# Chunk-select attention and a gated feed-forward on one core: the first group of gate weights in one transfer, 56 constant matmuls for 30, and a new order for the first 24 microseconds

## The chip, the core and the metric

The kernel runs on one core of one Trainium2 chip. A core has five engines with queues of their own: TensorE (PE, matmul; its weight loads are listed as PEld and overlap with the matmuls), VectorE (DVE), ScalarE (ACT), GpSimd (POOL) and SyncE (SP, which here only issues transfers). The metric is the device time of the program in microseconds, where less is better. A profiled execution also gives the start and the length of every instruction.

## What is computed

The first half is attention in which each query sees only the six best of the 24 chunks of 32 keys, chosen by an upper bound from each chunk's smallest and largest key. The second half is a feed-forward with a sigmoid gate. The shapes are B = 4, H = 8, S = 768, D = 64; then 3072 tokens of 512 numbers with 1536 hidden ones.

```python
k_min = np.min(k_chunks, axis=3)
k_max = np.max(k_chunks, axis=3)
ub = np.sum(np.maximum(q[:, :, :, None, :] * k_min[:, :, None, :, :], q[:, :, :, None, :] * k_max[:, :, None, :, :]), axis=-1)
ub = np.where(causal, ub, -1000000000.0)
top_chunks = np.argsort(ub, axis=-1)[..., -top_k:]
scores = scale * np.matmul(q, k.transpose(0, 1, 3, 2))
...
scores = np.where(mask, scores, -1000000000.0)
...
attn = attn / (np.sum(attn, axis=-1, keepdims=True) + 1e-09)
return np.matmul(attn, v).astype(np.float32)
...
gate = 1.0 / (1.0 + np.exp(-(x @ w_gate)))
val = x @ w_val
return (gate * val @ w_out).astype(np.float32)
```

## The kernel before, in words

Tokens are handled in eight units, `u0` to `u7`, of 384 rows. `u0` holds the first block of 128 rows of batches 0, 1 and 2 (the fourth batch's first block comes later, in `u2`). In these blocks every query sees at most four chunks, so the function `first` computes plain causal attention for them. The units from `u1` on go through the choice of chunks (`choose`) and the attention over them (`attend`); `ffn` follows for each. The attention of one unit is interleaved with the feed-forward of the unit before it.

Nothing is scheduled while the program runs or by a compiler. Each piece of work is recorded with `plan.add` under a name, with the buffers that it reads and writes. A hand-written table, `ORDER` (from L96), lists all names in sequence, with the letter of the engine after each (`P`, `A`, `V`, `G`, `S` for PE, ACT, DVE, GpSimd and SyncE); each engine executes its own entries in that sequence, and a piece that must wait holds up all that stands behind it on its engine. `SLOTS` gives every buffer its place: PSUM has eight banks, so each tile there waits until the last reader of the bank's former tile is done. `TIES` has entries `a<b`: piece `a` waits for piece `b`, on another engine, though no data goes between them.

These names are used later on, in the order in which the work flows:

- `fl_*` (`keep_awake`, L589 to L595): a matmul of a constant tile with itself, 128 x 256. Nothing reads its result. `ones16` (L587) is its input.
- `kfT_b`, `qfT_b` (L709): four transposes each, which turn the keys and queries of block b; `kf16_b`, `qf16_b` cast the result (the helper `copy`: L452 on ACT, L454 on DVE, L456 on GpSimd). `scf` (L746) are the block's scores, `expf` (L751) the exponentials, `cmf` (L753, GpSimd) the causal mask, `pvf` (L760) the product with the values, `rzf` and `xf` (L766, L768, DVE) the division, `xpsf` (L775) the transposes back and `xTf` the copies into `xT_u0`, which `u0`'s feed-forward reads. `vc_b` casts the values of block b.
- For `u1`: `kn`, `qn` copy the landed keys and queries (`kq_u`) into the layout for turning, `kT`, `qT` (L795) turn them, and `kt`, `qf`, `hk`, `hq` are copies and casts of these. `kx0`, `kx1` (L681) and `kxf` (L719) take the smallest and the largest key of each chunk, and `kcr_u1`, `kcr_f` (L688) finish the ranges; `qm` (L695) is the positive part of the queries. `ub_u1` (L896, tiles `ube`, `ubo`) multiplies queries with ranges and so needs all of `qf`, `qm` and `kcr` of the unit.
- `epat` (L561, L566) is a pattern that marks the chunk of each key; eight copies of it (`hkp000` to `hkp111`, 64 x 1536) fill the rows next to the keys, so that the score matmul adds the mask of the chosen chunks.
- `wgp` (L610), `wg0` to `wg2` (L612), `wv0` to `wv2` (L613) and `wo0` to `wo2` (L618) are transfers of the weights, cast to 16 bits on the way, all issued by GpSimd on the queue that the profile calls q0. The inputs are issued by SyncE on q1. A group of weights is 512 columns of hidden numbers, 512 KB as the profile counts it; `wgp` is its first quarter of rows, in one transfer ahead of the other three quarters.
- `g_u0_*`, `v_u0_*` (L1259) are the feed-forward matmuls of `u0`, four to a piece, one for each quarter of the rows. `tanh` (L1271) makes the gate and `hg` (L1280) the product of the two.

The work around the change is the front: it runs from the first instruction to the point where `g_u0` and `ub_u1` have started. SyncE's order there is `k2_u1`, the keys and queries of the first blocks, the other keys and queries of `u1`, then `v_0_3`, `v_0_2`, `v_0_1`, and then the loads of `u2` and of the fourth first block.

## Time and profile before

| | us |
|---|---|
| three runs of the kernel before | 279.79, 280.38, 280.73 |
| median of these | 280.38 |
| the profiled execution, its own time | 279.88 |
| span of the profile, first to last instruction | 278.2 |

The span is 1.68 us under the profiled execution's own time, which also holds what lies around the first and the last instruction. Times in the profile count from the start of the span. A line of a timeline or of the chain reads: start, duration, engine, source line, operation, output and input, number of instructions in the run; in brackets, how long the engine was idle before it and what released it. In a line of groups the busy time and the mean duration of one in ns stand after the bar. In the lines of the DMA queues the columns are packets, MB and the share of the 16 DMA engines' time. A last column at a transfer is the time from its issue to its landing.

### The profile page before, as it was taken

The numbers are of one execution on the slowest core, as the hardware profiler recorded it, in microseconds if no ns is written. First come the engines' busy times: TensorE is split into PE (matmuls) and PEld (weight loads), VectorE is DVE, ScalarE is ACT, GpSimd is POOL, SyncE is SP. The second block draws the span as 40 slices with busy tenths as digits, with TensorE's granted clock in tenths as the row PEclk, the third lists the DMA queues.
The fourth block names the chain that finished last, engine by engine and source line by source line (L and its number), as shares of the span: only waits on it lengthen the run. The fifth ranks groups of instructions, "written<-read, shape, count | busy, mean of one in ns | idle before, by whom it ended". The sixth has DMA issues, their size and how long they took to land.

```text
span 278.2 us, 7566 instructions
## 1 busy us (share of the span) xinstructions
PE 269.2 (97%) x2806; PEld 189.3 (68%) x2806; DVE 231.2 (83%) x686; ACT 180.4 (65%) x386; POOL 163.1 (59%) x262
## 2 busy tenths in 40 slices
...
GB/s 157 258 281 204 207 217 208 220 179 202 187 217 189 142 183 188 145 161 125 164 157 114 68 85 17 40 0 3 73 77 2 1 83 127 2 1 2 151 2 152
DMA packets 131717, 34.70 MB, mean 125 GB/s; under 512 B 119776, under 2 KB 128736, under 8 KB 131680
## 3 DMA queue, kind: packets, MB, share of 16 engines
...
q8 instruction: 22, 0.36, 0.5%
q14 instruction: 15, 0.12, 0.1%
...
## 4 chain that ended last, share of the span: by engine, by line
PE 87%; DMA 6%; DVE 5%; SPq 1%; issue 0%; POOL 0%; DVEq 0%
PE v_u L1259 20%; PE g_u L1259 15%; PE sc_u L957 12%; PE o_u L1308 11%; PE p_u L1082 10%; PE pv_u L990 7%; DMA wg<-in_moe_w_gate_dram 5%; PE p_g_u L1191 5%; PE ube_u L896 3%; DMA kf<-in_k_dram 1%; DVE xf L768 1%; PE kfT L709 1%; PE qfT L709 1%; PE fl L591 1%; DVE kx_u L681 1%; DVE kcr L681 1%
## 5 line engine op out<-in xcount | busy, mean ns | idle before, releaser
L968 ACT ACTIVATE att_u<-sc_u 128x512 f16<-128x512 f32 (+3 forms) x184 | 86.9, 573 | 8.6 <-PE sc_u L957 7.3
L1259 PE MATMUL v_u<-xT_u,wv 128*128 128x384 f16 x384 | 72.4, 326 | 0.0
L1280 DVE SCALAR_TENSOR_TENSOR hg_u<-gate_u,v_u 128x384 f16<-128x384 f16 x96 | 51.2, 545 | 19.3 <-ACT gate_u L1271 9.7
L1271 ACT ACTIVATE gate_u<-g_u 128x384 f16<-128x384 f32 x72 | 35.1, 499 | 40.3 <-PE g_u L1259 35.1
L1259 PE MATMUL g_u<-xT_u,wg 128*128 128x384 f16 x288 | 56.0, 326 | 0.9 <-ACT xT_u L452 0.5
L1259 PEld LDWEIGHTS <-wv 128*128 128x128 f16 x384 | 36.2, 98 | 20.3 <-issue 0.2
L974 POOL TENSOR_SCALAR_AFFINE_SELECT att_u<-att_u 128x384 f16<-128x384 f16 (+1 forms) x56 | 28.0, 509 | 37.4 <-ACT att_u L968 16.4
L1259 PEld LDWEIGHTS <-wg 128*128 128x128 f16 x288 | 26.7, 98 | 18.3 <-DMA wg<-in_moe_w_gate_dram 1.8
L1308 PE MATMUL o_u<-wo,hg_u 128*128 128x512 f16 x144 | 34.3, 379 | 0.0
L990 PE MATMUL pv_u<-v,att_u 128*128 128x65 f16 x640 | 26.3, 193 | 0.0
L990 PEld LDWEIGHTS <-att_u 128*128 128x128 f16 x640 | 24.2, 98 | 2.9 <-issue 0.6
L1228 DVE TENSOR_TENSOR f_g_u<-p_g_u,f_g_u 128x192 f32<-128x192 f32 (+1 forms) x72 | 24.9, 383 | 1.0 <-PE p_g_u L1191 0.4
L957 PE MATMUL sc_u<-hqe,hke 128*128 128x128 f16 (+2 forms) x220 | 25.1, 243 | 0.0
L957 PE MATMUL sc_u<-hqo,hko 128*128 128x128 f16 (+2 forms) x220 | 24.1, 243 | 0.0
L1308 PEld LDWEIGHTS <-hg_u 128*128 128x128 f16 x144 | 13.7, 98 | 13.4
L957 PEld LDWEIGHTS <-hke 128*128 128x128 f16 x220 | 16.5, 98 | 4.9 <-issue 0.6
L957 PEld LDWEIGHTS <-hko 128*128 128x128 f16 x220 | 16.4, 98 | 4.4
L673 POOL CAST v<-v 128x512 f16<-128x512 f32 x23 | 14.4, 627 | 5.8 <-DVE qf_u L863 1.8
L1271 ACT ACTIVATE gate_u<-f_g_u 128x384 f16<-128x384 f32 x24 | 11.9, 519 | 5.6 <-DVE hg_u L1280 2.9
L1011 DVE TENSOR_TENSOR x_u<-pv_u,rz_u 128x384 f16<-128x384 f32 (+1 forms) x28 | 14.6, 524 | 0.9 <-DMA xT_u<-x_u 0.6
L919 DVE MAX8 mx_u<-ubn_u 128x8 f32<-128x8 f32 (+16 forms) x152 | 12.7, 158 | 0.3
L1099 DVE SCALAR_TENSOR_TENSOR sw<-p_u,sw 128x256 f32<-128x256 f32 (+1 forms) x20 | 10.6, 528 | 2.4 <-PE p_u L1082 2.0
...
## 6 DMA issues: line engine op xcount, KB each, us to landing
...
qf<-in_q_dram SPq DMA_DIRECT2D x8, 128.0 KB, 3.3
```

The lines of the kernel that those rows point to most:

```text
L673: plan.add(f"v16_{b}_{ib}", {POOL: pool(H * D)}, lambda e: nc.gpsimd.tensor_copy(v16[b % 2][:, ib, :, 0:D], at(t)), reads=[t], writes=[("v ...
L957: nc.tensor.matmul(at(t)[:, o:o + 128 * m], hk[b % 2][e_][:, p, 128 * jb:128 * jb + 128], hq[u.side][e_][:, p, 128 * x:128 * (x + m)], sta ...
L968: plan.add(f"exp_{u.name}_{h}_{y}", {ACT: act(n)}, lambda e, t=t, att=att, b0=b0, n=n: nc.scalar.activation(at(att)[:, b0:b0 + n], at(t), ...
L974: nc.gpsimd.affine_select(out=dv, in_=dv, compare_op=ALU.is_ge, fill=0.0, base=0, pattern=[[0, u.m], [1, 128]], channel_multiplier=-1)
L990: nc.tensor.matmul(at(pv)[:, last, x, :], at(att)[:, c:c + 128], v16[b % 2][:, jb, h, :], start=(jb == 0), stop=(jb == ib))
L1011: plan.add(f"x_{u.name}_{p}", {DVE: dve(u.t)}, lambda e: nc.vector.tensor_tensor(at(x_).rearrange("p a (e d) -> p e a d", e=2), at(pv)[:, ...
L1082: nc.tensor.matmul(at(to)[:, side], a(j)[:, i], b(j)[:, i], start=j == i == 0, stop=j == 2 and i == 1)
L1228: plan.add(f"{p}_{name}", {POOL: pool2(192 * n), DVE: dve(192 * n)} if slow else {DVE: dve(192 * n)}, lambda e: both(e).tensor_tensor(dst( ...
L1259: nc.tensor.matmul(at(t), w16[:, c, 128 * fb:128 * fb + 128], at(u.xt)[:, c, :], start=(c == 0), stop=(c == 3))
L1271: plan.add(f"tanh_{u.name}_{fb}", {ACT: act(T, not seven[0])}, lambda e, gv=gv, gate=gate: nc.scalar.activation(at(gate), gv(), AF.Tanh, s ...
L1280: plan.add(f"hg_{u.name}_{fb}", {DVE: dve(T)}, lambda e, vv=vv, gate=gate, hg=hg, fb=fb: nc.vector.scalar_tensor_tensor(at(hg)[:, fb % 2], ...
L1308: nc.tensor.matmul(at(o), at(hgs[fc // 2])[:, fc % 2, 128 * tb:128 * tb + 128], wo16[:, fc, lo:hi], start=(fc == 0), stop=(fc == NFB - 1))
```

## The change

In the code, the loop that records the constant matmuls runs to 56. `wgp` is gone: `wg0` brings all four quarters, and the first four `g` pieces of a unit wait for it alone.

```diff
@@ -592,7 +596,7 @@
             at(t), ones16, ones16.unsqueeze(1).to_broadcast([128, 2, 128]), start=True, stop=True),
             reads=["ones16"], writes=[t], prio=-9.0)
 
-    for i in range(30):
+    for i in range(56):
         keep_awake(i)
     const("ident16", {DVE: (150, 230)}, lambda e: nc.vector.tensor_copy(ident16, ident32),
           reads=["ident32"], writes=["ident16"], prio=-1.0, port=True)
@@ -604,13 +608,8 @@
 
     def weights(i, prio, after):
         lo, hi = 512 * i, 512 * i + 512
-        c0 = 0
-        if i == 0:
-            c0 = 1
-            plan.add("wgp", {POOL: (760, 760)}, lambda e: nc.gpsimd.dma_start(wg16[:, 0:1, lo:hi], wgs[:, 0:1, lo:hi]),
-                     writes=[("wg", 0, "first")], prio=prio, dma=(750, 2048))
-        return plan.add(f"wg{i}", {POOL: (760, 760)}, lambda e: nc.gpsimd.dma_start(wg16[:, c0:, lo:hi], wgs[:, c0:, lo:hi]),
-                 reads=after, writes=[("wg", i)], prio=prio, dma=(750 * (4 - c0), 2048)), plan.add(f"wv{i}", {POOL: (760, 760)}, lambda e: nc.gpsimd.dma_start(wv16[:, :, lo:hi], wvs[:, :, lo:hi]),
+        return plan.add(f"wg{i}", {POOL: (760, 760)}, lambda e: nc.gpsimd.dma_start(wg16[:, :, lo:hi], wgs[:, :, lo:hi]),
+                 reads=after, writes=[("wg", i)], prio=prio, dma=(3000, 2048)), plan.add(f"wv{i}", {POOL: (760, 760)}, lambda e: nc.gpsimd.dma_start(wv16[:, :, lo:hi], wvs[:, :, lo:hi]),
                  reads=after, writes=[("wv", i)], prio=prio, dma=(3000, 2048))
 
     def weights_out(i, prio, after):
@@ -1265,7 +1264,7 @@
             else:
                 g = ps(f"g_{u.name}_{fb}", "ff", [128, T])
                 gv, gk = lambda g=g: at(g), [g]
-                op = plan.add(f"g_{u.name}_{fb}", pe(650), product(g, wg16), reads=xt + [("wg", fb // 4)] + [("wg", 0, "first")] * (fb < 4), writes=[g],
+                op = plan.add(f"g_{u.name}_{fb}", pe(650), product(g, wg16), reads=xt + [("wg", fb // 4)], writes=[g],
                               prio=next_())
                 plan.hold(op, gate)
             plan.add(f"tanh_{u.name}_{fb}", {ACT: act(T, not seven[0])}, lambda e, gv=gv, gate=gate: nc.scalar.activation(
```

The rest of the change lies in the three tables. In `ORDER` the entries up to the first score matmul of `u1` stand in a new sequence, here with the entries of before first; the 1770 behind them are the same, on the same engines. Of the pieces that both have, 25 change their engine; among them `hkp000` goes from ACT to DVE, `hkp100` from GpSimd to DVE, `hkf0` from GpSimd to ACT, `kf16_0`, `qf16_1` and `qf16_2` from DVE to ACT, and `kcr_f` from DVE to GpSimd. `hkp111` stays on ACT and moves to the end of this part. SyncE's transfers keep their sequence.

```diff
-ident=G ones16=V fl_4=P fl_2=P fl_8=P fl_3=P fl_1=P fl_0=P fl_29=P k2_u1=S kn_u1_2=A qf1_0=S kf1_0=S kf0_0=S fl_6=P fl_5=P epat0=V
-ident16=V ap0=V epat=G hkp110=A hkp000=A hkp001=V kT_u1_2=P kcr0=V kt_u1_2=V hk0_u1_2=G vf1_1=G hkp011=V hkp010=G vf1_2=G hkp100=G
-kf1_2=S kf0_1=S kfT_0=P kxf1=V fl_17=P fl_10=P fl_7=P kx0_u1_2=V kf16_0=V qf0_0=S qfT_0=P qf16_0=V qf1_1=S kf1_1=S kfT_1=P
-kf16_1=V fl_15=P fl_16=P scf_0=P expf_0_1=A fl_19=P qf0_1=S qfT_1=P hq0=V ap1=V fl_14=P fl_9=P fl_13=P fl_11=P fl_18=P fl_12=P
-qf16_1=V scf_1=P v10=G vf_0=S v16_0_0=G qf0_2=S qf1_2=S kf0_2=S expf_0_0=A cmf_0_0=G pvf_0_0=P rzf_0_0=V xf_0_0=V kx1_u1_2=V
-cmf_0_1=G wgp=G kfT_2=P pvf_0_1=P qfT_2=P qf16_2=V rzf_0_1=V xf_0_1=V kxf0=V expf_1_0=A cmf_1_0=G vf_1=S vc_1=G pvf_1_0=P
-rzf_1_0=V xpsf_0_0=P expf_1_1=A cmf_1_1=G pvf_1_1=P hkf0=G hk1_u1_2=A kf16_2=A scf_2=P expf_2_1=A expf_2_0=A k0_u1=S kn_u1_0=V
-kT_u1_0=P xf_1_0=V fl_20=P fl_21=P wg0=G q3_u1=S qn_u1_3=A q2_u1=S rzf_1_1=V xf_1_1=V xpsf_1_1=P hq1=V xTf_1_1=V kx0_u1_0=V
-kx1_u1_0=V vf_2=S wv0=G cmf_2_0=G fl_23=P xpsf_0_1=P fl_24=P fl_22=P fl_27=P xpsf_1_0=P vc_2=G xTf_1_0=V pvf_2_0=P rzf_2_0=V
-xf_2_0=V q1_u1=S k3_u1=S kn_u1_3=G kT_u1_3=P hkp111=A q0_u1=S fl_28=P kx1_u1_3=V cmf_2_1=G pvf_2_1=P xpsf_2_0=P rzf_2_1=V xf_2_1=V
-qT_u1_3=P qf_u1_3=V k1_u1=S qn_u1_1=A qT_u1_1=P xTf_0_0=A xTf_0_1=A qn_u1_2=A qn_u1_0=A kn_u1_1=G kT_u1_1=P kx1_u1_1=V kx0_u1_1=V
-kt_u1_0=A qm_u1_3=A fl_25=P xpsf_2_1=P fl_26=P qT_u1_2=P v_0_3=S v_0_2=S v_0_1=S qf1_3=S k0_u2=S q2_u2=S k1_u2=S qf_u1_1=V
-qf_u1_2=V v11=G wv1=G wg1=G hq0_u1_3=G qT_u1_0=P kt_u1_3=A hk0_u1_3=G hq1_u1_3=G wv2=G xTf_2_1=A xTf_2_0=A qf_u1_0=A qm_u1_0=A
-g_u0_0=P g_u0_2=P kx0_u1_3=V kcr_f=V kcr_u1=V hkp101=V hq1_u1_0=V hkf1=V kt_u1_1=V hk0_u1_1=G wg2=G qm_u1_2=A qm_u1_1=A ub_u1=P
-ubn0_u1=V ubm0_u1=V hq0_u1_1=A hq0_u1_2=A g_u0_3=P g_u0_1=P mx0_u1=V ap0_u1=V apt0_u1=V hqm0_u1_0=V v_u0_1=P v_u0_0=P v_u0_2=P
-hq0_u1_0=A tanh_u0_2=A tanh_u0_1=A hg_u0_1=V ubn1_u1=V v_u0_3=P tanh_u0_3=A hg_u0_3=V ubm1_u1=V hg_u0_2=V tanh_u0_0=A hg_u0_0=V
-hk0_u1_0=A hq1_u1_1=A sc_u1_0_2=P exp_u1_0_2=A sc_u1_1_2=P sc_u1_0_1=P sc_u1_0_0=P exp_u1_1_2=A sc_u1_1_0=P sc_u1_1_1=P
...
+ones16=V fl_17=P fl_6=P fl_15=P fl_39=P fl_36=P fl_2=P fl_14=P fl_33=P fl_31=P fl_34=P fl_5=P fl_10=P fl_32=P fl_1=P fl_35=P
+fl_19=P fl_16=P fl_21=P fl_7=P fl_3=P fl_0=P fl_37=P fl_30=P fl_4=P fl_13=P k2_u1=S qf1_0=S kf1_0=S kf0_0=S fl_54=P fl_27=P
+ident=G kfT_0=P ap1=V kcr0=V epat0=V epat=G hkp110=A hkp010=G hkp001=V hkp011=V vf1_1=G v10=G kf1_2=S kf0_1=S kf16_0=A qf0_0=S
+fl_9=P fl_8=P fl_29=P qfT_0=P qf16_0=V fl_52=P fl_47=P kn_u1_2=G kT_u1_2=P kx1_u1_2=V kt_u1_2=V hk0_u1_2=V ident16=V qf1_1=S
+kf1_1=S kfT_1=P hkf0=A scf_0=P expf_0_1=A expf_0_0=A cmf_0_0=G qf0_1=S fl_46=P qfT_1=P fl_50=P qf16_1=A fl_48=P fl_11=P fl_24=P
+fl_12=P fl_38=P vf_0=S v16_0_0=G qf0_2=S qf1_2=S qfT_2=P qf16_2=A kf0_2=S kf16_1=V fl_40=P scf_1=P fl_18=P pvf_0_0=P ap0=V
+hkp100=V cmf_0_1=G expf_1_0=A cmf_1_0=G expf_1_1=A vf_1=S vc_1=G rzf_0_0=V hq0=V kxf1=V kxf0=V xf_0_0=V fl_42=P kfT_2=P pvf_0_1=P
+fl_51=P fl_41=P fl_45=P fl_20=P fl_49=P xpsf_0_0=P pvf_1_0=P fl_26=P kf16_2=A cmf_1_1=G hkp000=V rzf_0_1=V wg0=G vf1_2=G wv0=G
+k0_u1=S kn_u1_0=A fl_28=P scf_2=P fl_22=P pvf_1_1=P rzf_1_1=V xf_1_1=V fl_55=P xpsf_1_1=P q3_u1=S q2_u1=S qn_u1_2=A kT_u1_0=P
+rzf_1_0=V xf_1_0=V xf_0_1=V qn_u1_3=V vf_2=S expf_2_0=A cmf_2_0=G expf_2_1=A q1_u1=S hk1_u1_2=G cmf_2_1=G k3_u1=S kn_u1_3=A
+kT_u1_3=P kx0_u1_2=V kx1_u1_0=V kx1_u1_3=V fl_23=P vc_2=A pvf_2_0=P rzf_2_0=V xf_2_0=V kx0_u1_0=V fl_44=P qn_u1_1=A qT_u1_3=P
+qf_u1_3=A hq0_u1_3=G q0_u1=S xpsf_1_0=P xpsf_0_1=P xTf_0_1=A pvf_2_1=P qT_u1_2=P qf_u1_2=A fl_25=P qT_u1_1=P rzf_2_1=V xf_2_1=V
+xTf_0_0=A xTf_1_1=A kt_u1_0=V k1_u1=S kn_u1_1=G kT_u1_1=P qf_u1_1=V qm_u1_1=A qm_u1_2=A xpsf_2_0=P xTf_2_0=A qn_u1_0=G v_0_3=S
+v_0_2=S v_0_1=S qf1_3=S k0_u2=S q2_u2=S k1_u2=S wv1=G hq1_u1_1=G wg1=G wv2=G xpsf_2_1=P xTf_2_1=V xTf_1_0=V kx0_u1_3=V kx0_u1_1=V
+kx1_u1_1=V kcr_u1=V fl_43=P fl_53=P qm_u1_3=V kcr_f=G wg2=G kt_u1_3=A qT_u1_0=P qf_u1_0=A qm_u1_0=A hkp101=V hq0_u1_2=A hk0_u1_3=A
+g_u0_2=P g_u0_0=P tanh_u0_0=A hq0_u1_0=A hq1_u1_0=G kt_u1_1=V hk0_u1_1=G hq1_u1_3=G hq0_u1_1=G ub_u1=P ubn0_u1=V ubm0_u1=V
+mx0_u1=V ap0_u1=V apt0_u1=V hqm0_u1_0=V g_u0_1=P tanh_u0_1=A tanh_u0_2=A g_u0_3=P v_u0_1=P hg_u0_1=V hkf1=V ubn1_u1=V v_u0_3=P
+tanh_u0_3=A hg_u0_3=V ubm1_u1=V hq1=V v_u0_2=P hg_u0_2=V v_u0_0=P hg_u0_0=V hk0_u1_0=A hkp111=A sc_u1_0_2=P exp_u1_0_2=A
```

`SLOTS` gives 712 buffers another place and has 26 new lines for the new `fl`; the tables' other entries stay. `TIES` has six more entries:

```diff
+hkp010<epat0 hq0_u1_3<xf_2_0 kn_u1_1<rzf_2_1 qn_u1_0<xf_2_1 kcr_f<kcr_u1 hq1_u1_0<hkp101
```

511 lines of the change are left out of this document (257 added, 254 removed).

## The prediction

> **What bounds the kernel now.** I read the page first: busy times, the clock, the chain that ended last.
>
> ```profile
> span 278.2 us, 7566 instructions
> PE 269.2 (97%) x2806; PEld 189.3 (68%) x2806; DVE 231.2 (83%) x686; ACT 180.4 (65%) x386; POOL 163.1 (59%) x262
> ...
> PE 87%; DMA 6%; DVE 5%; SPq 1%; issue 0%; POOL 0%; DVEq 0%
> ```
>
> TensorE (PE) is busy for 97% of the span and makes 87% of the chain. An average hides stages, so next came the busy time of each engine by stretches (after the two times: PE, weight load, DVE, ACT, POOL, each with its count; granted clock, DMA share, GB/s):
>
> ```profile
> 10.00:15.00 5.00, 4.23 (x47) 3.32 (x44) 3.29 (x9) 3.18 (x6) 3.79 (x7) 1.00 1.08 277
> 15.00:20.00 5.00, 3.72 (x47) 2.53 (x46) 4.65 (x16) 3.85 (x8) 4.85 (x9) 1.00 1.19 292
> 20.00:25.00 5.00, 4.37 (x48) 2.95 (x52) 4.92 (x14) 4.92 (x14) 4.05 (x8) 1.00 1.22 204
> 25.00:30.00 5.00, 5.00 (x53) 2.81 (x36) 4.24 (x20) 3.13 (x8) 3.12 (x5) 1.00 1.22 200
> 30.00:40.00 10.00, 10.00 (x91) 6.50 (x88) 5.87 (x24) 8.10 (x20) 5.36 (x11) 1.00 1.21 214
> 40.00:50.00 10.00, 9.75 (x118) 7.18 (x117) 6.34 (x17) 8.80 (x25) 5.21 (x11) 1.00 1.21 210
> ```
>
> Two regimes. From 25 us on PE is full but for 0.25 us between 40 and 50. Before 25 us PE has holes, DVE is full from 15 on, and ACT from 20 on. The change reorders only the work in front of the first feed-forward matmuls (and adds to it); the 1770 entries of the order behind it keep their sequence and their engines. So the end can move by three things alone: when the full stretch starts, whether the 0.25 us goes, and whether a new hole opens in it. The two ends of the front, and the hole (start, duration, instructions, idle before them with its releaser):
>
> ```profile
> 22.82 1.76 PE L1259 MATMUL g_u<-xT_u,wg 128*128 128x384 f16 x8 [0.51 <-ACT xT_u L452]
> 23.27 0.93 PEld L1259 LDWEIGHTS <-wg 128*128 128x128 f16 x7 [1.12 <-DMA wg<-in_moe_w_gate_dram]
> 24.51 0.10 PEld L896 LDWEIGHTS ube_u<-qf_u,kcr 64*32 64x32 f32 x1 [0.32 <-ACT qm_u L695]
> ...
> 40.45 1.48 PE L1259 MATMUL g_u<-xT_u,wg 128*128 128x384 f16 x8 [0.25 <-DMA wg<-in_moe_w_gate_dram]
> ```
>
> The first gate matmul starts at 22.82, when ACT has copied the last transposed block; its second needs the gate weights of the other rows, and the weight load waits for them to 23.27. At 24.51 the bounds product (L896) follows, which wants all key ranges, from DVE, and all range inputs, from ACT (the last of these released it). In the chain of waits stands DVE:
>
> ```profile
> 22.29 0.93 DVE qf_u L454 x2
> 23.21 0.47 DVE kcr L681
> 23.68 0.24 DVE kcr L688 x2
> ```
>
> The chain shows these pieces back to back to 23.92. The front is thus set by DVE, ACT and the transfer of the gate weights, within some half a microsecond of each other.
>
> **The change part by part.** *56 constant matmuls for 30.* PE runs slowly at first, as the same matmul shows early and late:
>
> ```profile
> 1.12 2.10 PE L591 MATMUL fl<-ones 128*128 128x256 f16 x9 [1.12 <-DVE ones L587]
> 5.81 1.09 PE L709 MATMUL kfT<-ident,kf 128*128 128x128 f32 x4 [0.90 <-DMA kf<-in_k_dram]
> 11.43 1.01 PE L591 MATMUL fl<-ones 128*128 128x256 f16 x6
> 12.89 0.63 PE L709 MATMUL kfT<-ident,kf 128*128 128x128 f32 x4
> ```
>
> Four transposes take 1.09 us at 5.81 and 0.63 at 12.89. Nine constant matmuls in 2.10 us are about 0.21 each, six in 1.01 about 0.12 (the last one's own time taken off). The new order puts 27 of them ahead of the first transposes, where nine stood: 27 x 0.21 = 5.7, so the slow rate all through ends them at 6.9 and the transposes at 8.0, against 6.90 before. If the unbroken run brings the faster rate after half of it, they end near 5.2, the transposes wait for their keys until 5.81 as now, and end at 6.4. The bounds of this part are -0.5 and +1.1 us on the first stage. I take +0.2, because the pieces of PE before lay apart and the rate still had not changed after six unbroken microseconds from 5.81. The Trainium skill ("TensorE: Matmul & The Clock Gate", Part 1) says that the array warms after a window of about 3.4 us of continuous activity, whatever the number of matmuls; the trace has 0.63 only much later, and by the rule this part would be the -0.5. The other 29 stand where 21 stood: eight more at 0.12, 1.0 us, in a stretch whose holes (10 to 25 us: 0.77 + 1.28 + 0.63) hold 2.7. They may shift a transpose by one's 0.12 at a time, and no sum of these; none stands behind 25 us.
>
> *The gate weights in one transfer.* GpSimd issues them:
>
> ```profile
> 12.82 0.79 POOL L610 DMA_DIRECT2D wg<-in_moe_w_gate_dram  x1
> ...
> 14.77 0.64 POOL L753 TENSOR_SCALAR_AFFINE_SELECT attf<-attf 128x512 f16<-128x512 f16 x1
> 15.35 0.61 POOL L456 COPY hke<-kf 64x512 f16<-64x512 f16 x1
> 15.91 0.80 POOL L612 DMA_DIRECT2D wg<-in_moe_w_gate_dram  x1
> ```
>
> One issue of 0.79 goes, and the copy of 0.61 ahead of the second moves to ACT. The transfer now stands directly behind the mask at 14.77, so 14.77 + 0.64 - 0.79 = 14.6 us at the earliest (if GpSimd alone sets it), 15.4 if the mask is not earlier. Its landing: the 384 KB issued at 15.91 are there at 23.2, 7.3 us later. 128 KB more, at the 512 KB per 3.5 us that q0's 2.94 MB in 20 us (below) make, are 0.9: 14.6 + 7.3 + 0.9 = 22.8; alone on the engines from the start it would be near 21.3. Both lie ahead of the 22.82 at which the first gate matmul can run, so the weight load's wait to 23.27 goes: about -0.45 of PE's time behind 22.82, if the bounds product at 24.51 can follow as much sooner.
>
> *Work moved between DVE, ACT and GpSimd.* Durations by kind:
>
> ```profile
> L454 DVE CAST qf<-qfT 128x512 f16<-128x512 f32 x3 | 2.1, 692 | 0.7 <-PE qfT L709 0.7
> L454 DVE COPY qf_u<-qT_u 128x384 f32<-128x384 f32 x3 | 1.6, 545 | 0.0
> L454 DVE COPY hke<-epat 64x1536 f16<-64x1536 f16 x2 | 1.1, 554 | 1.7 <-POOL epat L566 1.7
> L452 ACT COPY hko<-epat 64x1536 f16<-64x1536 f16 x2 | 2.9, 1467 | 0.0
> L452 ACT CAST kt_u<-kT_u 128x384 f16<-128x384 f32 x2 | 0.9, 466 | 0.0
> L452 ACT COPY qf_u<-qT_u 128x384 f32<-128x384 f32 x1 | 0.5, 500 | 0.0
> L695 ACT ACTIVATE qm_u<-qf_u 128x320 f32<-128x320 f32 x4 | 1.7, 462 | 0.1
> ```
>
> Off DVE ahead of the bounds product go three casts of 0.69, three copies of some 0.55, and five small pieces of 0.16 to 0.36, in all 4.9 us; on it come two patterns (2 x 0.55), two copies and a cast of some 0.55, one range input and a short copy: 3.2. DVE so has 1.7 us less. What comes of it is decided by the order, walked through with these durations: DVE ends the last sums at about 23.7 (23.92 before), since their inputs, transposes at 20 to 21 us, depend on loads that keep their place on SyncE. On ACT, the last transposed block now stands behind two range inputs of 0.46 that wait for DVE's copy of about 21.7, and ends near 22.9 (22.8 before); a cast, a copy and the last range input follow, 0.47 + 0.50 + 0.46, to 24.3. On GpSimd the final small sum (kcr_f, 0.16) stands behind three weight issues of some 0.8 and a cast, and ends near 24.3. So each engine comes out within about 0.2 us of the 24.5 of before or ahead of it; I take -0.1 for the bounds product, with -1.4 (all of the relief but 0.3) and +0.6 as bounds. One pattern of 1.47 us on ACT moves from 17.7 us to just ahead of the first exponential; ACT is 3.13 of 5 busy from 25 to 30, and that hides it. With the cover gone it would cost up to 1.47.
>
> *Later transfers.* The weights share the engines with SyncE's loads, packet for packet:
>
> ```profile
> q1 hardware_dynamic: 1721, 0.62, 116.9%
> q0 software_dynamic: 9, 0.01, 2.7%
> ...
> q0 software_dynamic: 2965, 2.94, 86.5%
> q1 hardware_dynamic: 2965, 1.24, 33.7%
> ```
>
> The first pair is 17 to 19 us: SyncE's queue (q1) alone moves 860 packets per us. The second is 27 to 47 us: both move 148 per us. The weights' groups follow each other, so one that starts 1.3 us sooner brings the fourth sooner as well, and the 0.25 us at 40.45 goes: -0.25. The price is on q1, which leaves its 860 for 148 about 1.3 us sooner: some 900 packets later to do. If the share is equal from then on, the loads make most of it good in the time in which weights alone were moving; if they first stand still, they come up to 4 us late. The last one of the next unit:
>
> ```profile
> 35.85 1.67 SPq L636 DMA_DIRECT2D qf<-in_q_dram  x1
> qf<-in_q_dram SPq DMA_DIRECT2D x1, 128.0 KB, 15.4
> 52.68 0.60 PE L709 MATMUL qfT<-ident,qf 128*128 128x128 f32 x4
> ```
>
> It lands at 35.9 + 15.4 = 51.3 and is used at 52.68: 1.4 us of slack, so the cost is between 0 and 2.6. I take 0, as the loads issued ahead of it wait for buffers too and make lateness good. This slack is also a cap: a PE that comes much over 1.4 us sooner waits there.
>
> *The sum*, against the profiled execution (span 278.2, in all 279.88 us, 0.5 under the median of 280.38): first stage +0.2, hidden behind SyncE's transfers up to the front's end, 0; front -0.1; 40.45 us -0.25; later transfers 0. That is -0.35, or 279.5 for a profiled execution and 280.0 for the median. The weight load's 0.45 isn't added: it ends with the bounds product, already counted.
>
> **The rivals.** (1) *Late loads, slower.* The weights in one piece push SyncE's loads as above: place, the transposes at 46 to 53 us of the next unit; price, up to 2.6 less the 0.35, say +1.8, or 282.2; it decides once the transfer is issued before about 14.5 us, and 14.6 is my walk. For it speak the equal 2965 packets; against it that 512 KB leave when 128 and 384 did, and only 1.3 us sooner. The Trainium skill ("DMA: Bandwidth & Descriptors", Queues, rings and completion order) has the engines alternate between queues at the granularity of packets; the equal counts agree, and by it a queue with larger packets takes the larger share of bytes.
>
> (2) *A late front, slower.* The 27 matmuls stay slow and the transposes end 1.1 us later; or the range inputs wait longer on ACT, ahead of the last block. Price +0.6 to +1.1, about 281.2. For it: 0.21 each in the row at 1.12; against: DVE and ACT stood idle in that stage (3.29 and 3.18 busy of 5), so that much of it is taken up.
>
> (3) *The relief passes, faster.* DVE's 1.7 us go through to the bounds product, capped by the 1.4 of slack: -1.0 to -1.4 with the 0.25, or 279.1. For it: 4.65 and 4.92 of 5 on DVE, on the chain; against: the inputs of its last sums, and ACT's 24.3, which no relief of DVE moves by itself.
>
> (4) *It does nothing*: fixed loads on both sides of the front make every shift wait. The 280.4 lies within my forecast.
>
> **How the numbers follow.** The forecast (-0.35, its own range 279.4 to 281.0) has 0.49, rival 1 0.22, rival 2 0.11, rival 3 0.18. Within 0.3% (0.84 us, about what a measurement of this kernel can tell from no change) lies most of the forecast's part, 0.41; 0.06 of it falls on faster, 0.02 on slower. So faster 0.24, same 0.41, slower 0.35. The range reaches from rival 3's 278.8 to rival 1's 282.5; what lies outside is the tail of both.
>
> **What would show it.** The first transposes before 7 us; the first gate matmul at 22.7 to 23.0 with no wait of its weight load; the bounds product at 24.3 to 24.5; no idle time of PE for weights at 40; nothing else idle on PE from 25 us on. Wrong would be: idle time of PE released by a query or key transfer or its copy between 33 and 53 us (rival 1); the bounds product behind 25 (rival 2) or ahead of 23.6 (rival 3); or a different rate of PE behind 25 us.

## The result, and the profile after

| | before | after |
|---|---|---|
| median, 17 runs of each on the same chip (us) | 280.51 | 282.24 |
| lowest, highest | 279.79, 283.68 | 280.40, 286.81 |
| ratio of the times, 95% interval | | 1.0051 [1.0027, 1.0075] |
| the profiled execution, its own time; its span | 279.88; 278.2 | 282.91; 281.2 |

The changed kernel is slower by 0.5%, some 1.4 us. The ratio leaves out executions more than 1.5% above the fastest of the same kernel, which the median doesn't. Two repeats of the unaltered changed kernel stand among the experiments.

The page of the changed kernel: span, busy time of PE, and the shares of the chain that ended last.

```profile
span 281.2 us, 7622 instructions
PE 270.8 (96%) x2832; PEld 190.5 (68%) x2832; DVE 231.3 (82%) x684; ACT 180.9 (64%) x387; POOL 162.9 (58%) x262
...
PE 90%; DMA 5%; SPq 2%; DVE 1%; issue 0%; POOL 0%; DVEq 0%; POOLq 0%
```

PE is busy for 1.6 us more in a span that is 3.0 us longer, so it stands idle more. Where, the stretches show (columns as in the prediction: two times, PE, PEld, DVE, ACT, POOL, granted clock, DMA share, GB/s):

```profile
15.00:20.00 5.00, 3.19 (x40) 2.32 (x39) 4.24 (x13) 3.29 (x7) 3.04 (x7) 1.00 0.97 190
20.00:25.00 5.00, 2.71 (x23) 2.08 (x23) 2.52 (x8) 2.23 (x6) 2.50 (x5) 0.93 1.21 210
25.00:30.00 5.00, 5.00 (x48) 2.23 (x48) 3.58 (x12) 3.23 (x8) 4.55 (x10) 0.73 1.24 223
...
40.00:50.00 10.00, 10.00 (x118) 7.47 (x116) 7.28 (x19) 7.65 (x20) 3.34 (x8) 1.00 1.20 216
```

Between 20 and 25 us PE worked 2.71 us where it had worked 4.37, and every other engine was half idle too: all of them waited for something outside. From 25 to 30 PE is full, but at a granted clock of 0.73. In the last row the 0.25 us without work is gone, as forecast. The timeline of PE in the changed kernel shows the place (start, duration, instructions; idle before them and its releaser in brackets):

```profile
1.12 4.41 PE L595 MATMUL fl<-ones 128*128 128x256 f16 x27 [1.12 <-DVE ones L591]
5.41 0.63 PE L708 MATMUL kfT<-ident,kf 128*128 128x128 f32 x4
...
16.62 0.50 PE L794 MATMUL kT_u<-ident,kn_u 128*128 128x128 f32 x3
17.70 0.55 PE L794 MATMUL kT_u<-ident,kn_u 128*128 128x128 f32 x3 [0.57 <-ACT kn_u L456]
...
23.50 0.55 PE L794 MATMUL kT_u<-ident,kn_u 128*128 128x128 f32 x3 [2.23 <-POOL kn_u L460]
...
25.00 2.77 PE L1258 MATMUL g_u<-xT_u,wg 128*128 128x384 f16 x8
27.70 0.45 PE L895 MATMUL ube_u<-qf_u,kcr 64*32 64x320 f32 x1
```

And the chain of waits names what stands behind that hole of 2.23 us:

```profile
13.94 8.87 DMA kq_u<-in_k_dram
...
22.94 0.52 POOL kn_u L460
```

The bounds product starts at 27.70, before at 24.51: +3.19, and less the 0.25 at 40 us this is the 3.0 of the span. It splits in three. The transposes of `k1_u1`, at 20.70 before (row below), start 2.80 later, since the keys land at 13.94 + 8.87 = 22.81. From there to the first gate matmul pass 1.50, before 2.12: -0.62. The eight gate matmuls up to the bounds product take 2.70, before 1.69: +1.01, at the lower clock. This is one execution; the repeats show that the late `k1_u1` isn't its rule.

For comparison the kernel before between the transposes of `k0_u1` and those of `k1_u1`, in the same view:

```profile
16.65 0.55 PE L795 MATMUL kT_u<-ident,kn_u 128*128 128x128 f32 x3 [0.55 <-DVE kn_u L454]
17.04 0.38 PE L591 MATMUL fl<-ones 128*128 128x256 f16 x2
...
17.87 0.49 PE L591 MATMUL fl<-ones 128*128 128x256 f16 x3
...
18.75 0.29 PE L760 MATMUL pvf<-vh,attf 128*128 128x65 f16 x4 [0.28 <-POOL vh L456]
19.20 0.55 PE L795 MATMUL kT_u<-ident,kn_u 128*128 128x128 f32 x3 [0.16 <-POOL kn_u L456]
...
20.70 0.49 PE L795 MATMUL kT_u<-ident,kn_u 128*128 128x128 f32 x3
```

Before, the 2.5 us in which PE waits for `k3_u1` (the transposes at 19.20) hold six constant matmuls, six transposes of `xf` and a product; no hole is over 0.3 us. After, nothing stands there (16.62 to 17.70 in the rows above). The queues between 18 and 20 us, before:

```profile
q1 hardware_dynamic: 1784, 0.47, 101.8%
q0 software_dynamic: 78, 0.08, 25.1%
```

and after (packets, MB, share of the engines):

```profile
q0 software_dynamic: 243, 0.25, 83.0%
q1 hardware_dynamic: 169, 0.12, 24.6%
```

A packet of the weights holds an engine for 0.83 x 16 x 2 us / 243 = 0.109 us, one of SyncE's for 1.018 x 16 x 2 / 1784 = 0.018 in the view before. SyncE's queue moved 0.12 MB in the two microseconds in which it had moved 0.47. That the weights displace SyncE's packets does not account for all of it: between 16 and 18 us, with the keys outstanding, the two queues together fill only 60.6 + 24.8 = 85.4% of the engines' time. What else held the keys up stays open.

### The profile page after: what moved, and what is told of

Its sections match the earlier page's. It is cut to its first block, busy times and chain, and to the rows that moved or that the text cites. A ratio compares the mean times of both kernels' runs of the same rounds, so it can differ in the third digit from the quotient of the medians.

```text
span 281.2 us, 7622 instructions
## 1 busy us (share of the span) xinstructions
PE 270.8 (96%) x2832; PEld 190.5 (68%) x2832; DVE 231.3 (82%) x684; ACT 180.9 (64%) x387; POOL 162.9 (58%) x262
## 4 chain that ended last, share of the span: by engine, by line
PE 90%; DMA 5%; SPq 2%; DVE 1%; issue 0%; POOL 0%; DVEq 0%; POOLq 0%
PE v_u L1258 22%; PE g_u L1258 17%; PE sc_u L956 12%; PE o_u L1307 11%; PE p_u L1081 10%; PE pv_u L989 7%; PE p_g_u L1190 5%; DMA kq_u<-in_k_dram 3%; PE ube_u L895 3%; DMA qf<-in_q_dram 2%; SPq L635 1%; SPq L646 1%; PE qfT L708 1%; PE qT_u L794 1%; PE kT_u L794 1%
## 5 line engine op out<-in xcount | busy, mean ns | idle before, releaser
L1258 PE MATMUL g_u<-xT_u,wg 128*128 128x384 f16 x288 | 57.2, 332 | 0.0
L1258 PEld LDWEIGHTS <-wg 128*128 128x128 f16 x288 | 27.3, 99 | 17.4 <-issue 2.7
L956 PEld LDWEIGHTS <-hke 128*128 128x128 f16 x220 | 16.5, 98 | 4.9 <-issue 0.6
L1010 DVE TENSOR_TENSOR x_u<-pv_u,rz_u 128x384 f16<-128x384 f32 (+1 forms) x28 | 14.6, 524 | 0.8 <-DMA xT_u<-x_u 0.5
```

The source lines that it names most:

```text
L956: nc.tensor.matmul(at(t)[:, o:o + 128 * m], hk[b % 2][e_][:, p, 128 * jb:128 * jb + 128], hq[u.side][e_][:, p, 128 * x:128 * (x + m)], sta ...
L1010: plan.add(f"x_{u.name}_{p}", {DVE: dve(u.t)}, lambda e: nc.vector.tensor_tensor(at(x_).rearrange("p a (e d) -> p e a d", e=2), at(pv)[:, ...
L1258: nc.tensor.matmul(at(t), w16[:, c, 128 * fb:128 * fb + 128], at(u.xt)[:, c, :], start=(c == 0), stop=(c == 3))
```

## The experiments

Three things were thus in question: the weights in one transfer (what it does to SyncE's loads), the 56 constant matmuls and their places (and the clock), and the new places in the queues of DVE and ACT. All kernels compute everything; they differ by a few entries of `ORDER`. "At full clock" below means that a run's mean granted clock is at least 0.997. A stretch of 3.4 us at half clock takes 3.4 / 2 / 280 = 0.006 off that mean, and runs lie at such steps (1.000, 0.994, 0.988).

**The weights alone.** In the kernel before, the whole first group at the place of its first quarter (issue at 12.87), or at the place of the rest (issue at 15.73):

```diff
 b_merged_early
-cmf_0_1=G wgp=G kfT_2=P
+cmf_0_1=G wg0=G kfT_2=P
-fl_21=P wg0=G q3_u1=S
+fl_21=P q3_u1=S
 b_merged_same
-cmf_0_1=G wgp=G kfT_2=P
+cmf_0_1=G kfT_2=P
```

> The kernel before, with all of wg0 in one transfer at the place of wgp (issue 12.8 us); nothing else is changed. Theory: k3_u1, q0_u1 and k1_u1 share the engines with it and k1_u1 lands at 22 to 23 us instead of 19.41; a hole of PE in front of kT_u1_1, the clock falls behind it; median 281.8 to 283.5. Rival (the new order of the front is at fault, not the transfer): k1_u1 by 20 us, 280.2 to 280.9.

> The kernel before, without wgp and with all of wg0 in one transfer at the place of wg0 (issue about 15.1 us). Theory: its data flow from about 18.5 us, when k1_u1 is all but there, so k1_u1 lands by 19.5 us and wg0 at 23.3 to 24.0; median 280.2 to 281.0. Rival (one transfer of 512 KB is worse than 128 and 384 at any place): 281.5 or more, with k1_u1 behind 21 us.

`b_merged_early`: ratio 1.0034 [0.9994, 1.0074], median 284.40 of 280.22 to 285.86, beside 281.18 for the kernel before (six of the twelve runs lie above 285, and only the median counts them); `b_merged_same`: 1.0018 [0.9998, 1.0038], median 281.68. PE in the first of them, timeline:

```profile
21.95 0.55 PE L767 MATMUL kT_u<-ident,kn_u 128*128 128x128 f32 x3 [0.98 <-POOL kn_u L433]
```

and in the second:

```profile
24.27 1.79 PE L1231 MATMUL g_u<-xT_u,wg 128*128 128x384 f16 x8 [2.05 <-DMA wg<-in_moe_w_gate_dram]
```

Early, the transfer delays `k1_u1`, whose transposes come at 21.95 instead of 20.70. Later, the first gate matmul waits for all 512 KB until 24.27, while before it needed the first quarter alone. So one transfer brings a wait of its own at either place, without any other part of the change. In time that is clear for the early place alone, by the six runs above 285; the profile shown is of a run of 280.22, with the bounds product at 24.85. For the later place the interval still holds 1. The runs at 285 have no profile; what they wait for isn't known.

**The weights later in the changed kernel**, behind the last mask (issue at 18.47):

```diff
 a_late
-rzf_0_1=V wg0=G vf1_2=G wv0=G k0_u1=S
+rzf_0_1=V vf1_2=G k0_u1=S
-cmf_2_1=G k3_u1=S
+cmf_2_1=G wg0=G wv0=G k3_u1=S
```

> The changed kernel with wg0 and wv0 issued by GpSimd behind cmf_2_1 (about 17.5 us instead of 14.44). Theory (the early weights take the DMA engines from k1_u1): k1_u1 lands near 19.5 us instead of 22.81, the PE hole of 2.2 us ahead of kT_u1_1 goes, the granted clock stays at 1.00 from 25 to 30 us; wg0 lands at 23.5 to 24.5, so that the first gate matmul waits up to 1 us for it; median 280.5 to 281.3. Rival (the new order of the front or the one transfer of 512 KB, wherever it stands, is at fault): kT_u1_1 still starts behind 22.5 us, median 282 or more.

1.0136 [1.0097, 1.0176]. The keys are in time (`k1_u1` at 18.74), but the weights land at 25.10, later than I had expected, and PE waits for them:

```profile
25.15 2.52 PE L1235 MATMUL g_u<-xT_u,wg 128*128 128x384 f16 x8 [2.18 <-DMA wg<-in_moe_w_gate_dram]
```

**Filling the hole ahead of `k1_u1`** with 22 more constant matmuls, all in one PSUM bank, then over four:

```diff
 a_fill, a_fill4
-kn_u1_1=G kT_u1_1=P
+kn_u1_1=G fl_56=P fl_57=P fl_58=P ... fl_77=P kT_u1_1=P
```

> The changed kernel with 22 more constant matmuls (2.4 us) on PE ahead of kT_u1_1, where PE stood idle for 2.2 us. Theory (the hole costs twice: itself and a lower granted clock behind it): k1_u1 lands as late as before, the hole is filled, the first eight gate matmuls take 1.4 us instead of 2.77, clock 1.00 in all runs; median about 281, 1.0 to 1.4 us under the changed kernel's 282.24. Rival (the low clock has another cause than the idle time): 0.73 from 25 to 30 us again, median 282 or more.

> The changed kernel with 22 more constant matmuls ahead of kT_u1_1, as in a_fill, but turning over four PSUM banks instead of one: there each waited for the one before it (0.37 us each, 8.2 in all) and the clock fell to 0.50. Theory (a stretch in which PE works little takes the clock, not the hole alone): the 22 run at 0.11 us each in 2.4 us, the granted clock stays at 1.00 from 25 to 30 us, the first eight gate matmuls take about 1.4 us instead of 2.77; k1_u1 still lands behind 22 us; 1.0 to 1.5 us under the changed kernel, ratio to the kernel before 0.999 to 1.003. Rival (the clock falls for another reason): clock 0.7 again from 25 to 30 us, ratio 1.005 or more.

1.0286 [1.0263, 1.0309] and 1.0114 [1.0081, 1.0147]. In these executions `k1_u1` had landed at 19.88 and 18.70, so there was no wait to fill, and the 22 pushed everything back. One bank and four banks, timeline of each:

```profile
21.53 8.23 PE L574 MATMUL fl<-ones 128*128 128x256 f16 x22
```

```profile
22.44 2.63 PE L574 MATMUL fl<-ones 128*128 128x256 f16 x22
```

This contradicts the first reading: the late `k1_u1` of the one profile is no constant property of the change. `a_fill` also shows that constant matmuls that come 0.37 us apart on average do not hold the clock: it was granted at 0.51 from 25 to 30 us and 0.50 from 30 to 35.

**The changed kernel again**, unaltered, on two other chips:

> The changed kernel, unaltered, for a second profile. In a_fill4 the same front had k1_u1 at 18.70 us instead of 22.81, and the filling of the hole cost 2.4 us. Theory A (the late k1_u1 is the rule): it lands behind 21 us again, PE idle 2 us ahead of kT_u1_1. Theory B (it is one outcome of a race; what costs in most runs are smaller holes of PE and, in some, a stretch of 3.3 us at half the clock right behind them): k1_u1 lands before 20.5 us, PE has holes of 0.5 to 1.5 us between 14 and 25 us, and the runs fall into groups by the mean clock, 281.0 to 281.8 us at 1.000 and 1.0 to 1.6 us more for each 0.006 of clock lost. Ratio 1.003 to 1.008 under both.

> The changed kernel, unaltered, on the chip of the next three, for a profile that stands beside theirs (that of after_again was of an execution of 718 us). Theory B: first gate matmul between 23.3 and 25.0 us, bounds product between 25.0 and 27.7; the last transposed block (xTf_2_0 on ScalarE) ends behind the two range inputs qm_u1_1 and qm_u1_2; ratio 1.002 to 1.007. Theory A (k1_u1 late each time): k1_u1 behind 21 us.

0.9997 [0.9964, 1.0031] and 1.0045 [1.0011, 1.0078]. With the runs of the first result there are 40 on three chips (one of 720 us, the one profiled in the first repeat, left aside). Without the executions that the comparisons leave out their median is 281.8, against 281.0 for 147 runs of the kernel before: +0.8. At full clock it is 281.4 (20 runs) against 280.8 (62), +0.6; below it 282.2 (12) against 281.1 (85), +1.1. So runs at a lowered clock take 0.3 longer in the kernel before and 0.8 in the changed one, and the larger part of the loss, 0.6, is there without it. The clock falls no more often than before (12 of 32 runs against 85 of 147); what differs is the time that goes with it. These are groups of runs sorted by their clock, not an experiment. The profile of the third series, timeline of PE:

```profile
16.86 0.50 PE L771 MATMUL kT_u<-ident,kn_u 128*128 128x128 f32 x3
19.13 0.90 PE L771 MATMUL kT_u<-ident,kn_u 128*128 128x128 f32 x3 [1.77 <-ACT kn_u L433]
...
25.16 1.46 PE L1235 MATMUL g_u<-xT_u,wg 128*128 128x384 f16 x8 [0.51 <-ACT xT_u L433]
26.55 0.45 PE L872 MATMUL ube_u<-qf_u,kcr 64*32 64x320 f32 x1
```

and its stretches:

```profile
19.00:20.50 1.50, 1.37 (x10) 1.25 (x11) 0.50 (x2) 1.01 (x3) 0.77 (x2) 0.51 1.15 165
20.50:22.00 1.50, 1.50 (x13) 1.35 (x12) 1.10 (x5) 0.65 (x2) 0.11 (x1) 0.50 1.12 156
```

Here `k1_u1` came at 19.59, and yet the bounds product is 2.0 us late. The hole is now ahead of `k3_u1`'s transposes (1.77), these take 0.90 instead of 0.55, and all of PE's work to 22 us goes at half the clock. The transposes of `k3_u1` start as early as before (19.13, before 19.20), so the 2.0 us are lost behind them. At the end PE waits 0.51 for the last transposed block, which stands on ACT behind the two range inputs; in the kernel before it waited as long for ACT's copy. ACT in the same execution:

```profile
24.02 0.83 ACT L671 ACTIVATE qm_u<-qf_u 128x320 f32<-128x320 f32 x2 [0.28 <-DVE qf_u L435]
24.76 0.35 ACT L433 COPY xT_u<-xpsf 128x256 f16<-128x256 f16 x1
```

**The first quarter apart again**, in the changed kernel; then the same with the rest tied to a later piece of DVE:

```diff
 a_split
-cmf_0_1=G expf_1_0=A
+cmf_0_1=G wgp=G expf_1_0=A
 a_split_tie, against a_split
-rzf_0_1=V wg0=G vf1_2=G wv0=G k0_u1=S
+rzf_0_1=V k0_u1=S
-rzf_1_1=V xf_1_1=V
+rzf_1_1=V wg0=G vf1_2=G wv0=G xf_1_1=V
 TIES: + wg0<rzf_1_1
```

> The changed kernel with the first quarter of the gate weights as a transfer of its own (wgp) behind cmf_0_1, as in the kernel before; wg0 with the other three quarters at its changed place. Theory (the one transfer of 512 KB is what costs, as it can't start early without delaying k1_u1 nor late without being late itself): k1_u1 lands by 21 us, wg0 by 23.3, the hole of PE ahead of the gate matmuls is under 1 us, clock 1.00; ratio to the kernel before 0.997 to 1.002. Rival (the new order of the front costs by itself): ratio 1.004 or more, with a hole of PE over 1 us that no transfer ends.

> As a_split, but wg0 (three quarters) and wv0 wait for rzf_1_1 on VectorE, so that they are issued at 16.0 us as in the kernel before instead of some 15.2. Theory: k1_u1 lands by 19.8 us, wg0 at 23.2 to 23.8; the gate matmuls start at 22.8 to 23.2; ratio 0.996 to 1.001. Rival (the new order of the front costs by itself): ratio 1.004 or more.

1.0040 [1.0018, 1.0062] and 1.0030 [1.0011, 1.0048]. Splitting doesn't undo the loss. In both profiles the hole stands ahead of `k3_u1`'s transposes, with 1.72 and 2.27 us, and half the clock behind it. What did not occur with it are the longest executions (below).

**The constant matmuls alone**: 13 more at the start of the kernel before, and 18 of the 27 taken from the start of the changed one.

```diff
 b_fl
-hkp001=V kT_u1_2=P
+hkp001=V fl_30=P fl_31=P fl_32=P ... fl_42=P kT_u1_2=P
 a_fl9
-ones16=V fl_17=P fl_6=P fl_15=P ... fl_16=P fl_21=P fl_7=P
+ones16=V fl_7=P
```

> The kernel before with 13 more constant matmuls ahead of kT_u1_2, 22 in one row; nothing else is changed. Theory (the constant matmuls bring the fast rate of PE early, and that is hidden by the loads and by VectorE): the first transposes take 0.63 instead of 1.09 us and end near 6.4 us, the first gate matmul starts within 0.3 us of 22.82; ratio 0.998 to 1.001. Rival (the extra matmuls themselves cost the changed kernel its time): ratio 1.003 or more.

> The changed kernel without 18 of the 27 constant matmuls ahead of the first transposes, so that nine stand there as in the kernel before. Theory B (the early warm PE is idle too much afterwards and is set back to half the clock late in the front, where the transposes and gate matmuls set the end): the first transposes take 1.09 us again and end near 6.9 us; PE turns fast near 12 us; fewer runs show a clock under 0.997 than of after_again, ratio lower by 0.001 to 0.004. Rival (the constant matmuls at the start have no part in it): the ratio and the share of runs with a lower clock are those of after_again.

`b_fl`: 1.0014 [0.9988, 1.0040], no difference that shows, though the interval allows 0.4%; `a_fl9`: 1.0036 [1.0006, 1.0066]. So fewer early matmuls don't mend the new order, and that more slow the old one isn't shown. The profile of `b_fl` is not what I had expected: the transposes are fast, but the first gate matmul starts at 24.18 and not near 22.82. A hole of 1.18 ends at 14.92, the clock is at half from 16.5 to 19.5, and the keys of `k3_u1` are waited for again (1.34). So the old order, with the weights apart, can lose its clock and its front too. In `a_fl9` (timeline of PE) nine of them leave the first transposes slow again:

```profile
1.12 2.10 PE L569 MATMUL fl<-ones 128*128 128x256 f16 x9 [1.12 <-DVE ones L565]
5.62 1.09 PE L682 MATMUL kfT<-ident,kf 128*128 128x128 f32 x4 [2.40 <-DMA kf<-in_k_dram]
```

1.09 us where the changed kernel has 0.63: the 27 in a row are what brings the faster rate. That gain doesn't reach the end, for at `k0_u1`'s transposes the changed kernel (16.62) is where the old one was (16.65): a transfer sets that point. In `a_fl9` the blocks' work is late instead (`k0_u1`'s and `k3_u1`'s transposes stand back to back at 18.21), so the keys are waited for no longer; its largest hole between 15 us and the first gate matmul is 0.83, and 10 of its 11 runs are at full clock (one of 565 us left aside).

**The queue places on ACT and DVE**: the last transposed block ahead of two range inputs, and `kcr_f` back on DVE; `xf_0_0` ahead of three other pieces of DVE; all three.

```diff
 a_qm_kcr
-qf_u1_1=V qm_u1_1=A qm_u1_2=A xpsf_2_0=P xTf_2_0=A qn_u1_0=G
+qf_u1_1=V xpsf_2_0=P xTf_2_0=A qm_u1_1=A qm_u1_2=A qn_u1_0=G
-kx1_u1_1=V kcr_u1=V fl_43=P fl_53=P qm_u1_3=V kcr_f=G wg2=G
+kx1_u1_1=V kcr_f=V kcr_u1=V fl_43=P fl_53=P qm_u1_3=V wg2=G
 TIES: - kcr_f<kcr_u1
 a_xf
-rzf_0_0=V hq0=V kxf1=V kxf0=V xf_0_0=V fl_42=P
+rzf_0_0=V xf_0_0=V hq0=V kxf1=V kxf0=V fl_42=P
 a_three: both
```

> The changed kernel with qm_u1_1 and qm_u1_2 behind xTf_2_0 on ScalarE, and kcr_f on VectorE ahead of kcr_u1 as in the kernel before (its tie is left out). Theory C (these two places in the queues hold up the end of the front): the first gate matmul starts 0.5 to 0.9 us earlier against the end of the last transposes (xpsf_2_0) than in after_third, and waits for wg0 instead, if that lands behind 23.5; ratio lower by 0.001 to 0.003 than after_third. Rival (the transfers alone set the front's end): the first gate matmul waits for wg0 or k1_u1 as late as in after_third, ratio unchanged.

> The changed kernel with xf_0_0 directly behind rzf_0_0 on VectorE, ahead of hq0, kxf1 and kxf0 (1.4 us). Theory D (VectorE, full from 16 us on, passes that delay on): the holes of PE ahead of xpsf_0_0 (0.8 us) and xpsf_1_1 (0.5 us) shrink, but the sums are only moved; ratio within 0.001 of after_third. Rival (this hole is what lowers the clock): fewer runs under 0.997 and a ratio lower by 0.002 or more.

> Both edits together: a_qm_kcr and a_xf in one kernel. Theory C and D: bounds product at 24.3 to 25.0 us, ratio 0.999 to 1.003 to the kernel before. Rival (what costs is the transfer of 512 KB alone): the first gate matmul behind 24 us, released by wg0 or k1_u1, ratio 1.004 or more.

1.0061 [1.0035, 1.0086], 1.0031 [1.0005, 1.0057] and 1.0024 [1.0004, 1.0045]. In `a_three` PE reaches both ends of the front like the kernel before (timeline):

```profile
23.22 1.46 PE L1235 MATMUL g_u<-xT_u,wg 128*128 128x384 f16 x8
24.61 0.45 PE L872 MATMUL ube_u<-qf_u,kcr 64*32 64x320 f32 x1
```

24.61 against 24.51. Its five runs at full clock have a median of 280.7, that of the kernel before at full clock (280.8), where the unaltered change has 281.4. That would put the 0.6 down to the three places, but it isn't shown: kernels below with the same three places end at 282.0 and 282.1 in 22 runs at full clock, and `a_three` itself has seven of twelve runs below full clock, at a median of 282.1. A long hole need not take the clock either: this execution is at 1.00 throughout.

```profile
18.89 0.55 PE L771 MATMUL kT_u<-ident,kn_u 128*128 128x128 f32 x3 [1.63 <-ACT kn_u L433]
```

In the profiles of `a_qm_kcr` and `a_xf`, executions of 287.45 and 288.23 us, the front is nearly in time too, with one or two of the places alone (bounds product at 24.89 and 24.82, full clock in the front), and yet the spans are 285.7 and 286.5. The chain of waits of `a_xf` says why:

```profile
16.73 23.79 DMA v<-in_v_dram
...
41.01 0.61 POOL v L649
```

and PE in its timeline:

```profile
42.15 0.62 PE L966 MATMUL pv_u<-v,att_u 128*128 128x65 f16 x8 [5.25 <-POOL att_u L950]
```

The last values of the first unit, `v_0_1`, issued at 16.73, land at 40.52; their cast on GpSimd holds up the masks queued behind it, and PE idles for 5.25 us (4.87 in `a_qm_kcr`). The kernel before casts them at 33.48. In both executions the next weights follow at 21.61 and 21.71, and SyncE's queue moves 848 and 922 packets between 24 and 26 us; in `a_three`, with that issue at 22.18, the weights' queue runs nearly empty there (158 packets) and SyncE's moves 1403. That the earlier issue brings the late values is argued from these three profiles; no run tests it.

**Covering the hole.** The three places with the first quarter apart; the same with eight of the 27 constant matmuls, over three banks, moved into the wait for `k3_u1`; this cover without the split:

```diff
 a_split_three, against a_three
-cmf_0_1=G expf_1_0=A
+cmf_0_1=G wgp=G expf_1_0=A
 a_split_cover, against a_split_three; a_three_cover, against a_three
-ones16=V fl_17=P fl_6=P fl_15=P fl_39=P fl_36=P fl_2=P fl_14=P fl_33=P fl_31=P
+ones16=V fl_31=P
-kT_u1_0=P rzf_1_0=V
+kT_u1_0=P fl_17=P fl_6=P fl_15=P fl_39=P fl_36=P fl_2=P fl_14=P fl_33=P rzf_1_0=V
```

> a_three with the gate weights split again (wgp behind cmf_0_1, wg0 with three quarters). Theory E (with one transfer of 512 KB SyncE's value loads v_0_3 to v_0_1 lose the engines to the weights at 17 to 24 us; if the next group of weights follows without a gap, v_0_1 lands near 40 us, PE idles 5 us and the run takes 286 us or more): no run over 284.5 us of twelve, as in a_split and a_split_tie; runs at a clock of 1.000 at 280.3 to 281.0 us, ratio 0.999 to 1.003. Rival (the slow runs come of the faster front alone): two or more of twelve over 286 us.

> a_split_three with eight of the 27 constant matmuls at the start moved between kT_u1_0 and kT_u1_3, where PE idled 0.6 to 2.3 us for the keys k3_u1. Theory F (that hole, which the kernel before filled with six constant matmuls and four transposes, is what takes the clock): the share of runs under a clock of 0.997 falls from about a half to a quarter or less, ratio 0.997 to 1.001. Rival (the clock falls whatever stands there): the share stays at a half, ratio within 0.001 of a_split_three.

> a_three, with the weights in one transfer, and the same eight constant matmuls moved as in a_split_cover. Theory F: fewer runs under 0.997 than a_three's 7 of 12. Theory E: the front ends earlier, wv1 is issued near 22 us and one run in six or more takes over 286 us, with v_0_1 behind 36 us. Rival to E: none over 286 us.

1.0051 [1.0024, 1.0078], 1.0024 [0.9999, 1.0049] and 1.0027 [0.9998, 1.0056]. Runs at full clock: 1 of 12 without the cover and 12 of 12 with it in the split pair; 5 of 12 and 10 of 12 in the other. `a_split_cover`, timeline of PE:

```profile
17.13 0.50 PE L776 MATMUL kT_u<-ident,kn_u 128*128 128x128 f32 x3
18.01 1.03 PE L572 MATMUL fl<-ones 128*128 128x256 f16 x8 [0.38 <-DVE xf L749]
19.55 0.55 PE L776 MATMUL kT_u<-ident,kn_u 128*128 128x128 f32 x3 [0.51 <-ACT kn_u L433]
```

and two stretches of `a_split_three`, whose hole at this place is 1.41:

```profile
19.00:20.50 1.50, 1.50 (x12) 1.38 (x11) 0.85 (x3) 0.55 (x2) 0.00 (x0) 0.50 1.19 193
20.50:22.00 1.50, 1.50 (x14) 1.26 (x12) 1.10 (x4) 0.80 (x2) 0.56 (x2) 0.61 1.20 197
```

Where no long hole is left the clock stays, here as in `a_fl9` (0.83 is the largest in both profiles between 15 us and the first gate matmul). Both kernels also have fewer constant matmuls at the start, 19 and 9 for 27, and no run separates that from the hole. What the half clock costs in the front can be read from this pair of profiles:

```profile
18.67 0.90 PE L776 MATMUL kT_u<-ident,kn_u 128*128 128x128 f32 x3 [1.41 <-ACT kn_u L433]
24.02 1.46 PE L1240 MATMUL g_u<-xT_u,wg 128*128 128x384 f16 x8
```

From these transposes to the first gate matmul `a_split_three`, at half clock, takes 24.02 - 18.67 = 5.35 us, and `a_split_cover`, at full clock, 23.89 - 19.55 = 4.34: 1.0 us. In time the cover's gain is 282.55 against 282.06, less than the two intervals can separate. In the profile of `a_three_cover` the keys were later, the hole was 1.49 despite the cover, and the clock fell.

**More work ahead of `k3_u1`**, as in the order before: `vc_2`, a product, four transposes back and two more constant matmuls.

```diff
 a_split_vc, against a_split_cover
-k3_u1=S kn_u1_3=A kT_u1_3=P kx0_u1_2=V kx1_u1_0=V kx1_u1_3=V fl_23=P vc_2=A pvf_2_0=P rzf_2_0=V xf_2_0=V
+k3_u1=S vc_2=A kn_u1_3=A fl_23=P fl_44=P xpsf_1_0=P xpsf_0_1=P pvf_2_0=P kT_u1_3=P kx0_u1_2=V kx1_u1_0=V rzf_2_0=V xf_2_0=V kx1_u1_3=V
```

> a_split_cover with three queues reordered, so that what needs no k3_u1 stands ahead of what waits for it: vc_2 ahead of kn_u1_3 on ScalarE; fl_23, fl_44, xpsf_1_0, xpsf_0_1 and pvf_2_0 ahead of kT_u1_3 on PE; rzf_2_0 and xf_2_0 ahead of kx1_u1_3 on VectorE, as in the kernel before. Theory G (in runs with a full clock the new order costs because vc_2, pvf_2_0, xf_2_0 and with them the last block of xT_u0 stand behind the keys k3_u1, which land at 18 to 19.6 us): from the start of kT_u1_3 to the first gate matmul 3.5 to 3.9 us instead of 4.34 in a_split_cover, ratio 0.998 to 1.001, all or nearly all runs at a clock over 0.997. Rival (the end of the front hangs on kT_u1_3 and the queries behind it alone): 4.2 us or more, ratio as a_split_cover's 1.0024.

1.0019 [0.9996, 1.0042], median 281.72, all 12 runs at full clock. From `k3_u1`'s transposes to the first gate matmul it now takes 23.18 - 19.25 = 3.93 us, in `a_split_cover` 4.34 and in the kernel before 22.82 - 19.20 = 3.62. The gain ends at the weights, for which the other seven matmuls wait to 23.85:

```profile
23.85 1.31 PE L1240 MATMUL g_u<-xT_u,wg 128*128 128x384 f16 x7 [0.34 <-DMA wg<-in_moe_w_gate_dram]
```

No version of the changed order beat the kernel before.

Part of what is left lies behind 25 us. In six of these profiles (`a_fill4`, `a_split`, `a_three`, `a_split_three`, `a_split_cover`, `a_three_cover`) PE stands idle for 0.36 to 0.45 us among the first scores of `u1`, waiting for DVE; the kernel before has no such hole. On DVE the copy `hkf1`, which ran at 24.80 in the kernel before, stands directly ahead of the piece that is waited for in all six (at 30.64, 0.38 us long, in `a_split_cover`, where the wait ends at 31.61). Other profiles with the same order have no such hole, and no run moved the copy back.

**Executions of over 286 us.** The kernels with the first quarter apart and the new order (five of them) had none in 61 runs, with a highest of 283.65. The changed kernel had 8 in its 40, `a_xf` 4 of 13, `a_qm_kcr` 2 of 8, `a_three` 1 of 12; `a_fl9` in 11 and `a_three_cover` in 12 had none. In the old order they are rare: 2 in 169 runs of the kernel before, 1 of 12 in `b_fl` and in `b_merged_same`. (`a_late`, `a_fill` and `a_fill4`, slower throughout, are left out.) The place is shown in two profiles, the late `v_0_1`; for the changed kernel itself no such execution was profiled, and the 1.0051 doesn't contain them.

## Why the prediction was right and wrong

I forecast 280.0, no change that can be measured, and the time is 282.24: inside the range, on the wrong side. The figure 282.2 is that of rival 1, but not the place that it names. In place, and over the runs on all three chips (+0.8) in size too, the outcome is rival 2, a late front at 281.2, to which I had given 0.11.

- *The first stage, +0.2 (bounds -0.5 and +1.1).* Wrong in sign and outside its bounds: the first transposes end at 5.41 + 0.63 = 6.04, before at 6.90. The lower bound let them wait for their keys to 5.81, and they begin at 5.41. (By the two rates that I used, a row that is fast from its middle on ends near 5.6 and not at 5.2; it ended at 1.12 + 4.41 = 5.53.) I had carried over a slow rate from the unbroken work behind 5.81, in which four transposes at 10.58 still took 1.06; it did not hold for 27 constant matmuls in a row, which took 4.41 us, with the four transposes right behind them at 0.63. The Trainium skill's window of about 3.4 us ("TensorE: Matmul & The Clock Gate", Part 1), which I had set aside, agrees with the 27, and not with that other stretch; what sets the two apart no run shows. That this part hides behind SyncE's transfers was right: nothing of the 0.86 is left at 16.62.
- *The front, -0.1 (bounds -1.4 and +0.6).* This is the term that decided, and the step that failed: the bounds product comes at 27.70 and 26.55 in two profiles against 24.51, +3.2 and +2.0, and the loss over the runs at full clock is 0.6. I had walked the queues with every transfer in its old place and at full clock. In the one profile the keys of `k1_u1` landed at 22.81, and what follows them set the end. In the other `k3_u1` was as early as before, and from its transposes to the first gate matmul passed 25.16 - 19.13 = 6.03 us, before 3.62. Of these 2.4 us pairs of profiles give 1.0 for the half clock (5.35 against 4.34), 0.7 for the three places (6.03 against 5.35 in `a_split_three`, at half clock like it, but with the weights apart), and 0.41 for `vc_2` and what follows it, which now stand behind the wait for `k3_u1` and which I did not see (4.34 against 3.93). Each is the difference of one pair, and how the 0.6 of the runs at full clock divides is not shown.
- *The other constant matmuls, a 0.12 at a time.* The second step that failed. I costed them as filler that could go anywhere between 10 and 25 us, and left the clock out of the sum, at nothing and without a reason: those of before stood, with the transposes back, in the wait for `k3_u1`. Without them that wait is a bare hole of 0.57 and 1.77 us in the two profiles of the changed kernel (up to 2.27 in its variants), and where the hole is 1.41 or more, half the clock comes with it or within a microsecond of its end in all of these profiles but one (`a_three`), just where transposes and gate matmuls set the end. By the pooled runs that goes with 0.8 us in 12 of 32, 0.3 on average; the pair of profiles has 1.0. That it goes with the bare hole is supported by the place of the slow stretch and by the counts with the eight matmuls and without; that the longer run at the start has no part in it isn't shown, and `b_fl`, which adds such a run to the old order, lost its clock too.
- *The weights issued at 14.6, there at 22.8.* The issue came at 14.44. The landing came at 23.88, and at 23.5 in the repeat, 23.1 in `a_three`: 512 KB beside SyncE's queue need 8.3 to 9.4 us, not 8.2. So the weight load's wait does not go: the first gate matmul now needs all 512 KB, which `b_merged_same` shows by itself, and even apart the rest is waited for to 23.85 in `a_split_vc`. In the profile of the changed kernel the wait is unseen, since the block before it was later still.
- *DVE's relief (rival 3).* It did not pass: between 20 and 25 us DVE was busy for 2.52 instead of 4.92, as it waited for keys and PE.
- *40 us, -0.25.* Right: PE is full there.
- *Later transfers, 0; rival 1.* Mechanism right, place wrong. Leaving q1's 860 packets per us earlier does hurt, and my bound "if they first stand still" is what happened: 169 packets in 2 us, 40 in the repeat. But it strikes `k1_u1` and `k3_u1`, inside the front, and `v_0_1`, the last to be served in its unit, with 5 us of PE, and not the queries of the next unit. By the Trainium skill ("DMA: Bandwidth & Descriptors", Queues, rings and completion order) engines alternate between queues by packets. From 28 to 34 us the trace of `a_xf` agrees, with 930 packets of q0 and 915 of q1; between 18 and 20 us it doesn't, since SyncE's side then has far fewer.
- *The rest of the kernel unchanged.* Right in the profile after, which has no other hole on PE behind 25 us. In six profiles of its variants there is one of 0.36 to 0.45 us, behind the new place of `hkf1` on DVE, which I had not walked.

Not settled: why the granted clock also falls in 85 of 147 runs of the kernel before, where it costs little (none of these runs was profiled); how often `k1_u1` is late, and why; and why the covered kernels, 34 of 36 runs at full clock, still end at 281.7 to 282.1 and not at the 280.7 of `a_three`'s best runs. For `a_split_cover` the profile names two parts of it, a bounds product 0.77 later than before (25.28) and the 0.41 behind 25 us.
